# Gated linear attention and a SiLU block: scores computed in halves of a chunk, without the masked block from the ninth chunk on

## The chip, the cores and the metric

The kernel runs on one core of a Trainium2 chip. A core has a matrix engine (PE, whose weight loads are listed as PEld), a vector engine (DVE), an activation engine (ACT), a general engine (POOL) and a queue that issues DMAs (SP). Each takes its own list of instructions in order, and they meet at semaphores. Matmuls read operands from the on-chip memory SBUF and write to the accumulator memory PSUM, which has eight banks of 512 float32 columns on 128 partitions. The metric is device time of one execution in microseconds (us); lower is better.

## The reference

Two stages, all float32. The first is a recurrence for each of 4 x 8 batches and heads over 768 tokens, with head size 48:

```python
for t in range(S):
    state = alpha[:, :, t, :, None] * state + np.einsum('bhd,bhe->bhde', k[:, :, t], v[:, :, t])
    y[:, :, t] = np.einsum('bhd,bhde->bhe', q[:, :, t], state)
```

The second takes `y` as 3072 tokens of 384 features: `h = x @ w_in` (384 x 2048), `g = h * sigmoid(h)`, `g @ w_out` (2048 x 384). The weights arrive as 64-bit floats and are converted on the chip.

## The kernel before

**Chunks.** The tokens are cut into 24 chunks of C = 128 tokens with all 8 heads: 6 positions times 4 batches, position by position. Inside a chunk the recurrence is written as a masked product. With A the running product of alpha, k is multiplied by the decay from its token to the chunk's end (k', tile `kp`), q by the inverse of that (q', tile `qp`), and `scores = k'ᵀ q'` for each head, of which only the part with key token <= query token is wanted. A matmul gives all 128 x 128; DVE multiplies by a mask as it brings the scores from PSUM to SBUF. The state of a batch is decayed by the chunk's whole product and gets `k'ᵀ v` added.

**Layout.** Heads go in four pairs (NP = 4): pair j has head 2j on partitions 0 to 47 and head 2j + 1 on 64 to 111, tokens along the columns. So a score matmul has 48 rows, and the two heads of a pair use the two row halves of PE at once, each with its own PSUM bank (`ps[0]`, `ps[1]`).

**Stages of a chunk** (functions of the chunk's number n):
- `products` (L652): alpha, k, q are brought to this layout, for the first NA = 8 chunks by PE transposes (L669), later by DVE from a tile of 32-token blocks that twelve DMAs fill (`turned`, L650). A DVE scan (L674) runs backward over alpha and gives the decays in tile `u`; L681 multiplies k with it in place, so k' lies in `u`. Column 0 of each pair in `u` is the chunk's whole product (`c["all"]`).
- `quotient` (L688): clamp (`least`, L696), reciprocal (L697), forward scan (L699) into tile `p`, product with q (L704), so q' lies in `p`. In the first eight chunks it is called from `products`.
- `scores` (L706): eight matmuls (L715), two masked copies on DVE (L719), four PE transposes of k' (L723) with one ACT copy (L725), four ACT products that decay the state (L729).
- `values` (L734): transposed outputs by matmuls that use four tiles of 32 output rows at once (L749), 16 with the masked scores and 12 with the state and q'; an ACT copy (L754) puts them into `xt`.
- `states` (L755): 16 small matmuls (L764) and two DVE additions (L770).

`u` and `p` come from pools with two buffers each (`upool`, `ppool`). The five PSUM tiles of a chunk (two for scores, one each for L723, `values`, `states`) rotate over the three banks of `ps_a`.

**The second stage as filler.** The matmuls of the SiLU block are cut into `pieces`: plain products for the first two groups of 512 tokens (L807), a scheme with fewer multiplications and more additions for the others (L830 in, L928 out, with DVE additions at L844, L933 and ACT copies at L836), and one plain output block (L955). `fill(step, slot)` runs pieces until the work done reaches what is due at this point.

**Order.** The loop over `step` writes the stages down in program order: in step n first `scores(n-1)`, then `products(n)`, then `values(n-1)` and `states(n-1)`, then from the ninth chunk on `quotient(n)`, with a `fill` after each of the four slots. Each engine's list is made from this when the program is compiled: what is ready goes first by program order, so independent work can move ahead. A tile of a pool has to wait until the last reader of the buffer's earlier content is done. SP issues loads in such an order too; v is loaded two chunks ahead with one DMA (L479), the blocks of alpha, k, q (L465) one chunk ahead.

**Early buffers.** The pools `raw`, `upp` and `spare` (weights on their way, token tiles of the first eight chunks) are closed by `settle` once the weights are converted; the tiles of the later form (`turn`, the 32-token blocks, ...) take their place. `settle` is tried after slots 1 to 3 of a step from step 7 on.

**Check.** The kernel reads all inputs once more (`audit`, L639) to see whether the quotient form is safe; the result is needed by L1147, late in the program.

Of the kernel before, what the change touches and what calls it, by code (L numbers as in the profile page):

```python
# [8 lines left out]
F32 = mybir.dt.float32  # L9
# [3 lines left out]
AF = mybir.ActivationFunctionType  # L13
ALU = mybir.AluOpType
# [5 lines left out]
def general(  # L20
# [29 lines left out]
    NFT = DF // 128  # L50
    NT = B * NCH
    LEVELS = [1 << i for i in range(7)]
# [255 lines left out]
    for ci in range(NCH):  # L308
        chunks = list(range(ci * B, (ci + 1) * B))
        for pair in (chunks[0:2], chunks[2:4]) if ci == 0 else [[n] for n in chunks]:  # L310
# [10 lines left out]
            for n in pair:  # L321
                if n + NIN < NT:
                    load(n + NIN)
# [32 lines left out]
def quotients(  # L356
# [19 lines left out]
    nc = tc.nc  # L376
    pe, dve, act, gps = nc.tensor, nc.vector, nc.scalar, nc.gpsimd
    B, H, S, D = q.shape
    C = 128
    NCH = S // C  # L380
    NP = H // 2
# [2 lines left out]
    NKT = HD // 128  # L384
    NFT = DF // 128
    NT = B * NCH
    W = C + 1
    GB = 4
    NG = NT // GB
    HF = NFT // 2  # L390
# [4 lines left out]
    def pool(name, bufs=1, space=None):  # L395
        kw = {} if space is None else {"space": space}
        return ctx.enter_context(tc.tile_pool(name=name, bufs=bufs, **kw))

    PS = bass.MemoryType.PSUM
    consts = pool("consts")  # L400
    fix = pool("fix")
# [3 lines left out]
    gpool = pool("gpool", 6)  # L405
    opool = pool("opool", 2)
    rpool = pool("rpool")
    upool = pool("upool", 2)
    ppool = pool("ppool", 2)

    ps_a = pool("ps_a", 3, PS)
    banks = [pool(f"ps_m{i}", 1, PS) for i in range(3)]
# [5 lines left out]
    def ps_attn(n=C):  # L418
        return ps_a.tile([128, 512], F32, name="ps_a").rearrange("p (j c) -> p j c", c=n)
# [5 lines left out]
    ident = consts.tile([128, 128], F32, name="ident")  # L425
# [7 lines left out]
    spare = first.enter_context(tc.tile_pool(name="spare", bufs=1))  # L433
# [4 lines left out]
    NA = 2 * GB  # L438
# [8 lines left out]
    ctxs = {}  # L447
# [26 lines left out]

    def load_v(n):
        c = ctxs.setdefault(n, dict(zip(("ci", "b"), divmod(n, B))))
        rows = slice(c["ci"] * C, c["ci"] * C + C)
        t = c["v"] = vns[n % NV]
        nc.sync.dma_start(t[:, :, 0:D], v[c["b"], :, rows, :].transpose([1, 0, 2]))  # L479

    early = []
    wide = moe_w_in.dtype != F32
# [19 lines left out]

    seg = [(fix if i == 0 else spare).tile([128, NP * W + 1], F32, name=f"al{i}") for i in range(2)]
    inv = fix.tile([128, NP * W + 1], F32, name="inv")
    one = consts.tile([128, NP * W + 1], F32, name="one")
    gps.memset(seg[0], 0.0)
    gps.memset(one, 0.0)
    gps.memset(one[:, 0 : NP * W + 1 : W], 1.0)
    for t in [inv] + seg[1:]:
        gps.memset(t, 0.0)  # L510


    mask = consts.tile([128, C], F32, name="mask")
    gps.memset(mask, 1.0)
    gps.affine_select(mask, mask, pattern=[[1, C]], compare_op=ALU.is_ge, fill=0.0, base=0,
                      channel_multiplier=-1)

    st = [fix.tile([128, NP, 2, D], F32, name=f"st{b}") for b in range(B)]
    for t in st:
        gps.memset(t, 0.0)  # L520
    least = fix.tile([128, NT, NP], F32, name="least")

# [18 lines left out]
    for n in range(NV):  # L541
        load_v(n)
# [99 lines left out]
    xts, xcs, late = {}, {}, {}  # L642

    def tokens(t):

        return t[:, 1 : NP * W + 1].rearrange("p (j c) -> p j c", c=W)[:, :, 0:C]

    def turned(x, to):
        x = x[:, 32:].rearrange("p (g j d) -> p g j d", j=4, d=D)
        dve.transpose(to.rearrange("p g (b j) -> p g j b", j=4), x[:, :, :, 0:32])  # L650

    def products(n):  # L652

        c = ctxs[n]
        sg = seg[0 if late else n % 2]
        ps = {}

        for name in ("a", "k", "q"):
            if n >= NA:
                if name == "a":  # L660
                    turned(c[name], tokens(sg))
                continue
            if n < GB and name != "a":

                ps[name] = out_bank("kq".index(name), 512).rearrange("p (j c) -> p j c", c=C)
            else:
                ps[name] = ps_attn()
            for j in range(NP):
                pe.transpose(ps[name][:, j, :], c[name][:, 2 * j : 2 * j + 2, :], ident)  # L669
            if name == "a":  # L670
                act.copy(tokens(sg), ps[name])  # L671
        end = NP * W
        u = upool.tile([128, end + 1], F32, name="u")
        dve.tensor_tensor_scan(u[:, end - 1 :: -1], sg[:, end:0:-1], one[:, end:0:-1],  # L674
                               0.0, ALU.mult, ALU.add)

        kp = c["kp"] = u[:, 1 : end + 1].rearrange("p (j c) -> p j c", c=W)[:, :, 0:C]
        if n >= NA:
            ps["k"] = late["turn"].tile([128, NP, C], F32, name="turn")
            turned(c["k"], ps["k"])  # L680
        dve.tensor_tensor(kp, ps["k"], kp, ALU.mult)  # L681
        c["all"] = u[:, 0:end:W]
        if n >= NA:
            c["sg"] = sg
        else:
            quotient(n, sg, ps["q"])

    def quotient(n, sg=None, q=None):  # L688

        c = ctxs[n]  # L690
        if sg is None:
            if n < NA:
                return
            sg = c.pop("sg")
        end, iv = NP * W, inv
        dve.tensor_single_scalar(least[:, n, :], c["all"], 2.0**-64, ALU.max)  # L696
        dve.reciprocal(iv[:, 0:end:W], least[:, n, :])  # L697
        p = ppool.tile([128, end + 1], F32, name="p")
        dve.tensor_tensor_scan(p[:, 0:end], sg[:, 0:end], iv[:, 0:end], 0.0, ALU.mult, ALU.add)  # L699
        qp = c["qp"] = tokens(p)  # L700
        if q is None:
            q = late["turn"].tile([128, NP, C], F32, name="turn")
            turned(c["q"], q)
        dve.tensor_tensor(qp, q, qp, ALU.mult)  # L704

    def scores(n):  # L706
        c = ctxs[n]
        ci, b = c["ci"], c["b"]
        ps = [ps_attn() for _ in range(2)]


        for j in range(NP):
            for u in range(2):
                r = slice(64 * u, 64 * u + D)
                pe.matmul(ps[u][:, j, :], lhsT=c["kp"][r, j, :], rhs=c["qp"][r, j, :],  # L715
                          start=True, stop=True)
        g = c["g"] = work.tile([128, 2, NP, C], F32, name="g")
        for u in range(2):
            dve.tensor_tensor(g[:, u], ps[u], mask[:, None, :].to_broadcast([128, NP, C]), ALU.mult)  # L719
        if ci < NCH - 1:  # L720
            ps_k = ps_attn()
            for j in range(NP):
                pe.transpose(ps_k[:, j, :], c["kp"][:, j, :], ident)  # L723
            c["kn"] = work.tile([128, NP, C], F32, name="kn")
            act.copy(c["kn"], ps_k)  # L725
        if ci > 0:
            s = st[b].rearrange("p j u e -> p j (u e)")
            for j in range(NP):
                act.mul(s[:, j], s[:, j], c["all"][:, j : j + 1])  # L729

# [285 lines left out]
    conv_done = [0, 0]  # L1016
# [51 lines left out]
    done, bridged = 0, 0  # L1068
    STEPS = NT + 1
    SLOTS = 4  # L1070
# [31 lines left out]
    for step in range(STEPS):  # L1102
        stages = [[(scores, 1)], [(products, 0)], [(values, 1)], [(states, 1)]]
        if step < GB:

            stages = stages[1::-1] + stages[2:]
        elif step >= NA:
            stages = [[(scores, 1)], [(products, 0)], [(values, 1), (states, 1)], [(quotient, 0)]]
        for slot, group in enumerate(stages):
            for stage, lag in group:  # L1110
                n = step - lag
                if not 0 <= n < NT:
                    continue
                stage(n)
                if stage is values:
                    bridged = n + 1
                if stage is products and n + NIN < NA:
                    load(n + NIN)
                if stage is quotient and n + 1 < NT:
                    load(n + 1)  # L1120
                if stage is states and n + NV < NT:
                    load_v(n + NV)
            fill(step, slot)
            if step >= NA - 1 and slot > 0 and conv_done[1] == NFT and not late:
                settle()
    turns = 0
    while next(audits, 0) is None:
# [10 lines left out]
    for i, (x, op, bound, holds) in enumerate(checks):  # L1138
        e = ends[:, i : i + 1]
        dve.tensor_reduce(e, x, axis=AX, op=op)  # L1140
        dve.tensor_single_scalar(e, e, bound, holds)  # L1141
    good = work.tile([128, 1], F32, name="good")
# [1 line left out]
    go_on()  # L1144
    go_on()
    ps = ps_attn()[0:1, 0, 0:1]
    pe.matmul(ps, lhsT=good, rhs=mask[:, C - 1 : C], start=True, stop=True)  # L1147
    dve.tensor_single_scalar(small, ps, 127.5, ALU.is_ge)
    for _ in range(4):
        go_on()  # L1150
# [60 lines left out]
```

## Time and profile before

| | us |
|---|---|
| median of 5 runs (lowest to highest) | 573.2 (572.31 to 574.53) |
| the profiled execution's own time | 574.4 |
| its span, first to last instruction | 572.7 |
| matmuls L928 (two forms), sum of their busy time | 122.7 + 91.6 |
| matmuls L807, 128 x 256 | 89.8 |
| scores L715, 384 records | 28.6 |
| values L749, 768 + 480 records | 28.8 + 17.0 |
| DVE transposes L650, 48 | 18.1 + 17.9 + 17.7 |

The mean granted clock of PE is 0.991. A float32 matmul appears as two records, a transpose as one. Busy time of a line is the time in which at least one of its instructions ran; the mean of one is longer where several run side by side. A timeline merges neighbours of one line and gives start, length, engine, line, tiles and how many; an entry in brackets is idle time ahead of it and what ended it. In the list of DMA issues, vn takes 3.4 us from issue to landing, the 32-token blocks 2.3 to 2.8.

### The profile page before, as it was taken

To read this page: it belongs to the slowest core of one execution; us is meant where nothing else is said; L and a number is where in the kernel's file an instruction comes from. 1 tells how busy PE (TensorE), PEld (TensorE's weight loads), DVE (VectorE), ACT (ScalarE), POOL (GpSimd) and SP (SyncE) were. 2 spreads that over 40 slices of the span, in tenths; PEclk is the share of its full clock that TensorE was granted. 3 is DMA by queue.
4 is the path that set the end of the run, shared out by engine and by line. 5 is a ranking of instruction groups with operands and counts; after the bars stand their busy time and mean duration, and the time that the engine had idled before them with its cause. 6 is when DMAs were issued, how large, how long until landed. Compare 5 with 4: busy or idle time off the path is not lost. (4 is left out here: it accounts for less than half of the span.)

```text
span 572.7 us, 11703 instructions
## 1 busy us (share of the span) xinstructions
PE 553.2 (97%) x4770; PEld 490.9 (86%) x4770; DVE 449.2 (78%) x807; ACT 187.4 (33%) x367; POOL 7.3 (1%) x25
## 2 busy tenths in 40 slices
PE   5889999999999999999999999999999999999986
PEld 3777887678999999899999999999898999998986
DVE  5879799899798699996997996997962866756751
ACT  2345443233211232442433442423432341423100
POOL 5000000000000000000000000000000000000000
PEclk9799999999999999999999999999999999999998
DMA  9997785336434414443324332324210113333320
GB/s 213 170 289 216 201 215 135 94 97 152 115 91 122 128 46 104 129 112 81 109 56 129 113 106 77 114 50 113 64 39 15 52 52 117 117 96 126 97 76 28
DMA packets 93903, 63.77 MB, mean 111 GB/s; under 512 B 54800, under 2 KB 85520, under 8 KB 93840
## 3 DMA queue, kind: packets, MB, share of 16 engines
q1 hardware_dynamic: 93840, 62.94, 41.8%
q8 instruction: 39, 0.64, 0.5%
q14 instruction: 24, 0.20, 0.1%
HBM read 58.20 MB, written 4.72 MB: 110 GB/s over the span
## 5 line engine op out<-in xcount | busy, mean ns | idle before, releaser
L928 PE MATMUL ps_o<-w_out,g 128*128 128x192 f32 x704 | 122.7, 328 | 1.4 <-DVE o L942 1.3
L928 PEld LDWEIGHTS ps_o<-w_out,g 128*128 128x128 f32 x704 | 115.3, 190 | 4.3 <-DVE o L942 1.7
L928 PE MATMUL ps_o<-wt,g 128*128 128x192 f32 x528 | 91.6, 326 | 0.1
L807 PE MATMUL ps_m<-xt,w_in 128*128 128x256 f32 x384 | 89.8, 384 | 1.7 <-DVE w_in L604 1.0
L928 PEld LDWEIGHTS ps_o<-wt,g 128*128 128x128 f32 x528 | 87.2, 190 | 1.7 <-DVE u L1004 0.4
L807 PEld LDWEIGHTS ps_m<-xt,w_in 128*128 128x128 f32 x384 | 70.7, 190 | 13.1 <-DVE w_in L604 3.4
L830 PE MATMUL ps_m<-xc,w_in 128*128 128x256 f32 x288 | 70.1, 379 | 0.3 <-DVE g L844 0.3
L639 DVE TENSOR_REDUCE seen<-bits 128x1 f32<-128x384 int32 (+2 forms) x65 | 42.4, 689 | 26.6 <-DMA bits<-in_moe_w_out_dram 21.0
L830 PEld LDWEIGHTS ps_m<-xc,w_in 128*128 128x128 f32 x288 | 54.0, 190 | 6.8 <-DVE g L844 0.6
L830 PE MATMUL ps_m<-xc,wx 128*128 128x256 f32 x192 | 50.1, 383 | 0.0
L836 ACT COPY g<-ps_m 128x512 f32<-128x512 f32 x64 | 36.9, 586 | 39.1 <-PE ps_m L830 39.1
L933 DVE TENSOR_TENSOR g<-g 128x512 f32<-128x512 f32 x66 | 44.7, 687 | 4.7 <-PE ps_o L928 4.7
L841 ACT ACTIVATE g<-g 128x1024 f32<-128x1024 f32 x32 | 33.2, 1056 | 43.8 <-DVE g L844 43.8
L729 ACT ACTIVATE st<-st,u 128x96 f32<-128x96 f32 x80 | 25.9, 368 | 54.1 <-DVE u L674 38.9
L844 DVE TENSOR_TENSOR g<-ps_m,g 128x512 f32<-128x512 f32 x56 | 37.6, 682 | 2.9 <-PE ps_m L830 2.7
L830 PEld LDWEIGHTS ps_m<-xc,wx 128*128 128x128 f32 x192 | 35.0, 190 | 4.2 <-issue 0.4
L719 DVE TENSOR_TENSOR g<-ps_a,mask 128x512 f32<-128x512 f32 x48 | 31.2, 685 | 6.2 <-PE ps_a L715 5.9
L674 DVE TENSOR_TENSOR_SCAN u<-al,one 128x516 f32<-128x516 f32 x24 | 29.3, 1222 | 5.4 <-ACT al L671 5.4
L699 DVE TENSOR_TENSOR_SCAN p<-al,inv 128x516 f32<-128x516 f32 x24 | 29.5, 1229 | 4.8 <-PE ps_a L749 4.2
L836 ACT COPY part<-ps_m 128x512 f32<-128x512 f32 x32 | 18.7, 586 | 43.4 <-PE ps_m L830 38.1
L810 ACT ACTIVATE g<-ps_m 128x512 f32<-128x512 f32 x32 | 19.0, 593 | 41.0 <-PE ps_m L807 40.7
L749 PE MATMUL ps_a<-g,vn 128*32 128x128 f32 x768 | 28.8, 282 | 1.9 <-DVE g L719 1.9
(117 smaller groups left out, 630.6 us busy)
## 6 DMA issues: line engine op xcount, KB each, us to landing
bits<-in_moe_w_in_dram SPq DMA_DIRECT2D x24, 512.0 KB, 4.1
bits<-in_moe_w_out_dram SPq DMA_DIRECT2D x32, 384.0 KB, 3.2
at<-in_alpha_dram SPq DMA_DIRECT2D x64, 96.0 KB, 2.3
kt<-in_k_dram SPq DMA_DIRECT2D x64, 96.0 KB, 2.8
qt<-in_q_dram SPq DMA_DIRECT2D x64, 96.0 KB, 2.6
vn<-in_v_dram SPq DMA_DIRECT2D x24, 192.0 KB, 3.4
bits<-in_alpha_dram SPq DMA_DIRECT2D x9, 512.0 KB, 3.6
out_dram<-o SPq DMA_DIRECT2D x48, 96.0 KB, 1.8
```

The lines of the kernel that those rows point to most:

```text
L639: dve.tensor_reduce(seen[kind][which][:, i : i + 1], x, axis=AX, op=op, apply_absolute_value=True))
L674: dve.tensor_tensor_scan(u[:, end - 1 :: -1], sg[:, end:0:-1], one[:, end:0:-1], 0.0, ALU.mult, ALU.add)
L699: dve.tensor_tensor_scan(p[:, 0:end], sg[:, 0:end], iv[:, 0:end], 0.0, ALU.mult, ALU.add)
L719: dve.tensor_tensor(g[:, u], ps[u], mask[:, None, :].to_broadcast([128, NP, C]), ALU.mult)
L749: pe.matmul(py[32 * at : 32 * at + 32, t, :], lhsT=w, rhs=x, start=(i < 4), stop=(i >= len(todo) - 4), skip_group_check=True)
L807: pe.matmul(ps[:, e, :], lhsT=w_in[:, t, (f + e) * 128 : (f + e + 1) * 128], rhs=xt[:, t, :], start=(t == 0), stop=(t == NKT - 1))
L830: pe.matmul(ps[:, e], lhsT=block_w(w)[:, 2 * pair + e], rhs=block_x(grp, x), start=(first and e == 0), stop=(e == 1), skip_group_check=True)
L836: act.copy(to, ps)
L841: act.activation(x, x, AF.Silu)
L844: dve.tensor_tensor(to, a, b, op)
L928: pe.matmul(ps, lhsT=x, rhs=w[:, i], start=(first and i == 0), stop=(i == HF - 1), skip_group_check=True)
L933: dve.tensor_tensor(cells(grp, h, pair, *to), cells(grp, h, pair, *x), cells(grp, h, pair, *y), ALU.subtract)
```

## The change

A score matrix has four blocks of 64 x 64, of which the one with late keys and early queries is masked off whole. The scores are now computed by sixteen matmuls with 64 keys each instead of eight with 128, and from the ninth chunk on those of the late keys stream the 64 late queries alone. For pairs 2 and 3 (four heads) the two halves of the keys change places: k' is written with its halves swapped, v is loaded with its halves swapped, and the mask has a second form. The PSUM cells that no matmul writes are set to zero by ACT beforehand (`blank`), since the masked copy reads them. k' no longer lies in `u` but in a tile of its own, so that the product with the decay is two instructions; k' and q' have two buffers in turn for the first eight chunks and one from then on. The clamp `least` moves to `products`, and the state's decay reads it. `settle` cannot come before the last slot of step 7.

```diff
-    upool = pool("upool", 2)
-    ppool = pool("ppool", 2)
+    upool = pool("upool")
...
-        nc.sync.dma_start(t[:, :, 0:D], v[c["b"], :, rows, :].transpose([1, 0, 2]))
+        nc.sync.dma_start(t[:, 0 : H // 2, 0:D], x[:, 0 : H // 2])
+        for e in range(2):
+            nc.sync.dma_start(t[CH * e : CH * e + CH, H // 2 :, 0:D], x[CH - CH * e : C - CH * e, H // 2 :])
...
+    kps = [(spare if i else fix).tile([128, NP, C], F32, name=f"kp{i}") for i in range(2)]
+    qps = [(spare if i else fix).tile([128, NP * W + 1], F32, name=f"p{i}") for i in range(2)]
+
+    def turns(x, n):
+
+        return x[(n + 1) % 2 if n < NA else 0]
...
-    mask = consts.tile([128, C], F32, name="mask")
+    mask = consts.tile([128, 2, C], F32, name="mask")
     gps.memset(mask, 1.0)
-    gps.affine_select(mask, mask, pattern=[[1, C]], compare_op=ALU.is_ge, fill=0.0, base=0,
-                      channel_multiplier=-1)
+    for odd in range(2):
+        for e in range(2):
+            m = mask[CH * e : CH * e + CH, odd, :]
+            gps.affine_select(m, m, pattern=[[1, C]], compare_op=ALU.is_ge, fill=0.0,
+                              base=-CH * (e ^ odd), channel_multiplier=-1)
...
-        kp = c["kp"] = u[:, 1 : end + 1].rearrange("p (j c) -> p j c", c=W)[:, :, 0:C]
+        dve.tensor_single_scalar(least[:, n, :], u[:, 0:end:W], 2.0**-64, ALU.max)
+        kp = c["kp"] = turns(kps, n)
+        ut = tokens(u)
...
-        dve.tensor_tensor(kp, ps["k"], kp, ALU.mult)
-        c["all"] = u[:, 0:end:W]
+        j = NP // 2
+        dve.tensor_tensor(kp[:, 0:j], ps["k"][:, 0:j], ut[:, 0:j], ALU.mult)
+        k, ut = [x[:, j:].rearrange("p j (e c) -> p j e c", e=2) for x in (ps["k"], ut)]
+        dve.tensor_tensor(kp[:, j:].rearrange("p j (e c) -> p j e c", e=2)[:, :, ::-1], k, ut, ALU.mult)
...
-        dve.tensor_single_scalar(least[:, n, :], c["all"], 2.0**-64, ALU.max)
         dve.reciprocal(iv[:, 0:end:W], least[:, n, :])
-        p = ppool.tile([128, end + 1], F32, name="p")
+        p = turns(qps, n)
...
+    def blank(n):
+
+        if n < NA:
+            return
+        ps = ctxs[n]["blank"] = [ps_attn() for _ in range(2)]
+        for t in ps:
+            act.activation(t.rearrange("p j c -> p (j c)"), ident[:, 0:1].to_broadcast([128, 4 * C]),
+                           AF.Copy, scale=0.0)
...
-        for j in range(NP):
-            for u in range(2):
-                r = slice(64 * u, 64 * u + D)
-                pe.matmul(ps[u][:, j, :], lhsT=c["kp"][r, j, :], rhs=c["qp"][r, j, :],
-                          start=True, stop=True)
+        for j in (0, 2, 1, 3):
+            for e in range(2):
+                for u in range(2):
+                    r = slice(64 * u, 64 * u + D)
+                    at = slice(CH * e, CH * e + CH)
+                    t = slice(CH * (e ^ j // 2) if n >= NA else 0, C)
+                    pe.matmul(ps[u][at, j, t], lhsT=c["kp"][r, j, at], rhs=c["qp"][r, j, t],
+                              start=True, stop=True)
...
-            dve.tensor_tensor(g[:, u], ps[u], mask[:, None, :].to_broadcast([128, NP, C]), ALU.mult)
+            dve.tensor_tensor(g[:, u].rearrange("p (o j) c -> p o j c", o=2),
+                              ps[u].rearrange("p (o j) c -> p o j c", o=2),
+                              mask[:, :, None, :].to_broadcast([128, 2, NP // 2, C]), ALU.mult)
...
-                act.mul(s[:, j], s[:, j], c["all"][:, j : j + 1])
+                act.mul(s[:, j], s[:, j], least[:, n, j : j + 1])
...
-            stages = [[(scores, 1)], [(products, 0)], [(values, 1), (states, 1)], [(quotient, 0)]]
+            stages = [[(scores, 1)], [(products, 0)], [(values, 1), (states, 1)], [(quotient, 0), (blank, 0)]]
...
-            if step >= NA - 1 and slot > 0 and conv_done[1] == NFT and not late:
+            if step * SLOTS + slot >= NA * SLOTS - 1 and conv_done[1] == NFT and not late:
                 settle()
```

CH is 64, half a chunk.

More of the change, by code (lines that the diff above doesn't have):

```diff
@@ L386, in quotients @@
     NT = B * NCH
+    CH = C // 2
     W = C + 1
@@ L476, in load_v @@
         c = ctxs.setdefault(n, dict(zip(("ci", "b"), divmod(n, B))))
-        rows = slice(c["ci"] * C, c["ci"] * C + C)
+        x = v[c["b"], :, c["ci"] * C : c["ci"] * C + C, :].transpose([1, 0, 2])
         t = c["v"] = vns[n % NV]
-        nc.sync.dma_start(t[:, :, 0:D], v[c["b"], :, rows, :].transpose([1, 0, 2]))
+        nc.sync.dma_start(t[:, 0 : H // 2, 0:D], x[:, 0 : H // 2])
+        for e in range(2):
+            nc.sync.dma_start(t[CH * e : CH * e + CH, H // 2 :, 0:D], x[CH - CH * e : C - CH * e, H // 2 :])
     early = []
@@ L708, in scores @@
         ci, b = c["ci"], c["b"]
-        ps = [ps_attn() for _ in range(2)]
-        for j in range(NP):
-            for u in range(2):
-                r = slice(64 * u, 64 * u + D)
-                pe.matmul(ps[u][:, j, :], lhsT=c["kp"][r, j, :], rhs=c["qp"][r, j, :],
-                          start=True, stop=True)
+        ps = c.pop("blank") if n >= NA else [ps_attn() for _ in range(2)]
+        for j in (0, 2, 1, 3):
[6 more added lines that the diff above has]
+                              start=True, stop=True)
         g = c["g"] = work.tile([128, 2, NP, C], F32, name="g")
         for u in range(2):
-            dve.tensor_tensor(g[:, u], ps[u], mask[:, None, :].to_broadcast([128, NP, C]), ALU.mult)
+            dve.tensor_tensor(g[:, u].rearrange("p (o j) c -> p o j c", o=2),
+                              ps[u].rearrange("p (o j) c -> p o j c", o=2),
+                              mask[:, :, None, :].to_broadcast([128, 2, NP // 2, C]), ALU.mult)
         if ci < NCH - 1:
@@ L1146, in quotients @@
     ps = ps_attn()[0:1, 0, 0:1]
-    pe.matmul(ps, lhsT=good, rhs=mask[:, C - 1 : C], start=True, stop=True)
+    pe.matmul(ps, lhsT=good, rhs=mask[:, 0, C - 1 : C], start=True, stop=True)
     dve.tensor_single_scalar(small, ps, 127.5, ALU.is_ge)
```

## The prediction

> **What bounds the kernel now.** I read the page's busy shares first, then the busy time by stretch, then the timeline of one step, then the waits.
>
> Page, part 1 and the head of part 5:
> ```profile
> span 572.7 us, 11703 instructions
> PE 553.2 (97%) x4770; PEld 490.9 (86%) x4770; DVE 449.2 (78%) x807; ACT 187.4 (33%) x367; POOL 7.3 (1%) x25
> ```
> Busy time of each engine in stretches of 40 us (columns PE, PEld, DVE, ACT, POOL, clock, DMA):
> ```profile
> 160.00:200.00 40.00, 40.00 (x390) 36.52 (x389) 31.66 (x60) 9.20 (x20) 0.00 (x0) 1.00 0.45 121
> 200.00:240.00 40.00, 39.28 (x308) 35.46 (x306) 39.65 (x78) 12.95 (x28) 0.00 (x0) 1.00 0.33 92
> 280.00:320.00 40.00, 40.00 (x394) 36.84 (x393) 35.55 (x65) 14.77 (x27) 0.00 (x0) 1.00 0.34 93
> ```
> PE has no idle time in most of the middle, at full clock. So whatever PE time goes away in a late step should leave the total, unless the next engine is late. That engine is DVE: 79 to 89% busy, and 99% from 200 to 240, the one stretch with PE stalls (0.72 us).
>
> Timeline of PE over one step (start, length, line):
> ```profile
> 305.51 1.08 PE L749 MATMUL ps_a<-g,vn 128*32 128x128 f32 x32
> 306.41 0.84 PE L749 MATMUL ps_a<-p,st 128*32 128x128 f32 x24
> 307.07 0.52 PE L764 MATMUL ps_a<-vn,kn 128*32 128x48 f32 x32
> 307.52 1.13 PE L830 MATMUL ps_m<-xc,wx 128*128 128x256 f32 x4
> ...
> 315.50 1.16 PE L715 MATMUL ps_a<-p,u 48*128 48x128 f32 x16
> 316.59 0.66 PE L723 MATMUL ps_a<-ident,u 128*128 128x128 f32 x4
> ```
> A float32 matmul stands as two records. L749 packs four 32-column tiles: 24 records are 6 rounds of four and take 307.07 - 306.41 = 0.66, so 0.110 us per round of 128 columns. The scores (L715) pack two row halves: 16 records are 8 rounds, 0.88 us at that rate, yet the next line starts 1.09 us later. The other 0.21 us lies around the change of tile shape, before and after.
>
> **The change, part by part.**
>
> *Scores on PE.* Eight matmuls with 128 stationary columns become sixteen with 64, so four tiles (two row halves, two column halves) take part. In the first eight chunks each tile still streams 4 x 128 columns in two records each: 8 rounds, nothing gained. From the ninth on, a tile streams 128, 64, 128, 64: in rounds 2 x (1 + 1/2 + 1 + 1/2) = 6, if a tile goes on to its next matmul while its neighbour still streams. Then the stage takes 6 x 0.110 + 0.21 = 0.87 us, 0.22 less, over 16 chunks 3.5 us. If tiles go in step, each round has a long member and nothing is saved. The rows nearest to that question are early ones in which 48-column and 128-column matmuls of the same tile shape overlap:
> ```profile
> 24.66 0.30 PE L749 MATMUL ps_a<-g,vn 128*32 128x128 f32 x3
> 24.70 0.21 PE L764 MATMUL ps_a<-vn,kn 128*32 128x48 f32 x1
> 24.74 0.86 PE L749 MATMUL ps_a<-g,vn 128*32 128x128 f32 x23
> 25.34 0.29 PE L764 MATMUL ps_a<-vn,kn 128*32 128x48 f32 x4
> 25.43 0.27 PE L749 MATMUL ps_a<-g,vn 128*32 128x128 f32 x1
> 25.43 0.21 PE L764 MATMUL ps_a<-vn,kn 128*32 128x48 f32 x1
> ```
> Four short ones start between 25.34 and 25.43 while long ones are still under way and another long one starts after them. A tile that goes at its own pace does this; tiles in step would not. I take 3.5, with 0 as the other end.
>
> A rule speaks against it. The Trainium skill, "TensorE: Matmul & The Clock Gate", Part 3 (row and column tiling), says that matmuls are strictly first-in first-out, in start and in end. By that a tile that is free early waits for the earlier instruction to start: with the written order of heads (0, 2, 1, 3) the last tile ends after 7 rounds, the gain is estimated at 0.11 x 16 = 1.8 us, and the sum below would come to 572.7. The interleaved rows are nearer to the case, so I stay with 6 rounds.
>
> *Blanking.* Two ACT copies of 512 columns into PSUM per late chunk; such copies take 0.58 us (kn, L725), so 1.2 us per step of 21 on an engine that is 33% busy. They use banks whose last reader is ACT itself (kn, then xt), so ACT blocks on nothing new; they are written in front of a slot of filler work, which lasts 8 us on PE (307.52 to 315.50). Cost 0 while that cover stands; without it, up to 1.2 us per step. The wait of the first score for ACT adds at most one sequencer entry: 0.05 x 16 = 0.8; I count 0, the filler ahead covers it.
>
> *k times its decay in two halves (L681).* One 512-element product of 0.69 us becomes two of 256; xc rows of 256 take 0.41 and start 0.34 apart, so the pair holds DVE for about 0.68 where the one held 0.61: 0.07 x 24 = 1.7 us of DVE, beside PE except in the start and in the saturated stretch. The clamp (L696, 0.17) only moves ahead. The mask product has the same element count: 0.
>
> *Buffers.* k' gets a tile of its own, and from the ninth chunk k' and q' have one buffer each instead of two. So the k' product waits for the transposes of the chunk before (L723, at the step's start; it is needed a whole step later: 0), and the quotient scan (L699) waits for the values of the chunk before, no longer of the one before that. Behind L699 on DVE are the q' product (L704) and all later DVE work of the fillers; scores wait for L704. From the end of L749 (307.3) to L715 (315.50) there are 8.2 us; scan and product need 1.23 + 0.69. In the worst step that I found, five microseconds of sums stand ahead:
> ```profile
> 284.35 0.84 PE L749 MATMUL ps_a<-p,st 128*32 128x128 f32 x24
> 290.71 1.23 DVE L699 TENSOR_TENSOR_SCAN p<-al,inv 128x516 f32<-128x516 f32 x1
> 292.17 0.69 DVE L704 TENSOR_TENSOR p<-turn,p 128x512 f32<-128x512 f32 x1
> 293.45 1.16 PE L715 MATMUL ps_a<-p,u 48*128 48x128 f32 x16
> ```
> There the product would end at 292.86, 0.6 us ahead of the scores. So the new wait just fits. I count 0.5 us for the whole run, from 0 to the rival's price.
>
> *v in three DMAs.* SP issues two more per chunk, 0.39 each, with 12 loads of 0.43, stores and reads of the audits in a step of 21 us: hidden, since v is loaded more than a step ahead. At the start four more stand in front of the third chunk's loads: 4 x 0.39 = 1.6 us. Bytes are the same, and the DMA engines are the limit there (busy share 9 tenths or more), so I take half, 0.8; ends 0 and 1.6. The four mask selects and the larger memset on POOL (0.29 each, about 1 us) end long before the first mask product at 14.7: 0.
>
> *Loads of the ninth chunk.* The close of the early buffers moves two slots later, and the region now holds q' of the seventh chunk, read until 107.3. Twelve loads of 0.43 after that are 5.2 us, plus 2.5 to land: about 115. The ninth chunk's q' cannot be written before the eighth's values end (121.9) anyway, and its scores start at 127.4: 0.
>
> Sum on the profiled execution: 574.4 (span 572.7 and 1.7 around it) - 3.5 + 0.8 + 0.5 = 572.2. That execution is 1.2 above the median of the runs, so the median goes from 573.2 to 571.0.
>
> **The rivals.**
>
> *The quotient comes late (slower).* Place: L699 to L704, in each of 16 steps. For it: DVE is 85% busy, and a queue in order puts other late products in front; the measured slack was 0.6 us at the worst step. Against it: 8.2 us of cover in a usual step, with 1.9 needed. It decides once PE waits more than 2.2 / 16 = 0.14 us per step; at 0.35 it costs 5.6 and gives 571.0 - 0.5 + 5.6 = 576.1.
>
> *DVE becomes the bound in its full stretches.* For it: 99% from 200 to 240 and 36.17 of 40 us from 360 to 400. Some 5.5 of 16 steps would then save nothing (1.2 us lost) and the 0.07 per chunk counts there (0.4): 572.6.
>
> *Tiles go in step.* The scores take 8 rounds as before; only the costs stay: 573.2 + 1.3 = 574.5. The rows at 25.34 speak against it, though they show 32-column tiles, not halves of rows and columns at once.
>
> **How the numbers follow.** Forecast as summed 0.52 (its own range 569.4 to 572.0: from all costs at 0 with 0.3 of luck in order, to 0.9 more); late quotient 0.20; DVE bound 0.18; tiles in step 0.10. A measurement of this kernel tells about 0.2%, 1.15 us, so faster means below 572.05 and slower above 574.35. Faster: nearly all of the forecast's 0.52 and a fifth of the DVE case, 0.55. Slower: the late quotient and half of the tiles in step, 0.25. The rest, 0.20. The range from 569.3 to 575.8 leaves out the far part of the late quotient and a little at the lower end.
>
> **What would show it.** Right: score records from the ninth chunk on start the transposes 0.87 us later, not 1.09; PE stays at 40 of 40 us; the scores' idle time names no DVE or ACT; the last scores start about 2 us sooner than 443.0. Wrong: PE idle ahead of the scores put down to L704 or to the blanking; 1.09 us still; a start of the third chunk more than 1.6 us later than 32.3; DVE above 99% in more stretches with PE below 40.

## The result and the profile after

The changed kernel takes 570.95 us (median of 28 runs, 569.73 to 573.56), the kernel before 573.37 (52 runs, 572.12 to 574.99): ratio 0.9963, 95% interval 0.9955 to 0.9971, 2.4 us less. The profiled execution's own time is 573.12 (span 571.4); that of the kernel before was 574.4.

Head of the page of the changed kernel:
```profile
span 571.4 us, 12612 instructions
PE 552.8 (97%) x5154; PEld 488.8 (86%) x5154; DVE 448.9 (79%) x831; ACT 201.9 (35%) x399; POOL 8.4 (1%) x28
```
PE is busy 0.4 us less than before and ACT 14.5 us more (for the most part the blanking copies). The stretches shown before, now (columns PE, PEld, DVE, ACT, POOL, clock, DMA):
```profile
160.00:200.00 40.00, 40.00 (x425) 36.57 (x425) 34.42 (x66) 11.24 (x25) 0.00 (x0) 1.00 0.44 118
200.00:240.00 40.00, 38.35 (x334) 34.37 (x332) 39.62 (x80) 14.08 (x29) 0.00 (x0) 0.98 0.39 109
280.00:320.00 40.00, 40.00 (x429) 36.89 (x428) 35.78 (x68) 18.01 (x35) 0.00 (x0) 1.00 0.36 94
```
PE is still full in the first and last, at full clock. In the middle one it has lost 0.93 us more than before, and the clock is no longer 1.00. The lines have moved: scores L715 to L745, transposes of k' L723 to L755, values L749 to L781, states L764 to L796, sums of the expert products L844 to L876.

The timeline of PE over the same late step:
```profile
306.52 0.84 PE L781 MATMUL ps_a<-p,st 128*32 128x128 f32 x24
307.18 0.52 PE L796 MATMUL ps_a<-vn,kn 128*32 128x48 f32 x32
...
315.61 0.90 PE L745 MATMUL ps_a<-p,kp 48*64 48x128 f32 x32
316.44 0.66 PE L755 MATMUL ps_a<-ident,kp 128*128 128x128 f32 x4
```
The scores' stage, from their first record to the next line, takes 316.44 - 315.61 = 0.83 us; before it took 1.09. All chunks from the tenth on show 0.83 (the ninth 0.95, with a wait of 0.20 ahead of it). In the fifth to eighth chunk, where nothing is left out, it takes 1.04:
```profile
97.28 1.10 PE L745 MATMUL ps_a<-p,kp 48*64 48x128 f32 x32
98.32 0.66 PE L755 MATMUL ps_a<-ident,kp 128*128 128x128 f32 x4
```

So the saving is there and no wait took its place at the scores. Where did it go? Compare the starts of the scores, changed minus before. At the fifth chunk (66 us) it is -0.22; at the ninth -0.20; from the tenth on each step adds -0.26, down to -1.39 at 226.37 (before 227.76). The fifteenth chunk's scores start at 251.10, 0.89 **later** than before; then -0.26 per step again down to -1.46 at the last (441.58 against 443.04). Between two steps 2.54 us were lost. The timeline of PE there:
```profile
236.90 1.13 PE L862 MATMUL ps_m<-xc,w_in 128*128 128x256 f32 x4 [1.24 <-DVE g L876]
238.43 1.97 PE L862 MATMUL ps_m<-xt,w_in 128*128 128x256 f32 x4 [0.40 <-DVE g L876]
```
The same two waits in the kernel before:
```profile
237.62 1.13 PE L830 MATMUL ps_m<-xc,w_in 128*128 128x256 f32 x4 [0.32 <-DVE g L844]
239.15 1.13 PE L830 MATMUL ps_m<-xt,w_in 128*128 128x256 f32 x4 [0.40 <-DVE g L844]
```
So PE stalls (stands idle) 0.92 us more. And the second row lasts 1.97 instead of 1.13 us: the granted clock is 0.5 for 3.41 us from 238.6, which costs 1.7. Stalls and clock together are about the 2.5 us. A second profile of the changed kernel, taken beside the later experiments, has the same two stalls and keeps its full clock there:
```profile
238.40 1.13 PE L862 MATMUL ps_m<-xc,w_in 128*128 128x256 f32 x4 [1.24 <-DVE g L876]
239.93 1.13 PE L862 MATMUL ps_m<-xt,w_in 128*128 128x256 f32 x4 [0.40 <-DVE g L876]
```
In it this step takes 23.11 us (scores to scores) where the first profile has 24.73, so the half clock cost 1.6. It also hides the saving in PE's busy time: of the 4.2 us that the scores save, the half clock takes back 1.7, and in the first 40 us PE is busy 2.0 us more than before (32.14 instead of 30.12).

Of the 32 executions of the changed kernel whose mean granted clock is on record beside this result, the 17 with 0.997 or more have a median of 570.6 us, the 15 with less 572.55. Where the clock was low in them is known only for the profiled one.

The step that the prediction called the worst, now (timeline of all engines):
```profile
286.44 1.23 DVE L716 TENSOR_TENSOR_SCAN p<-al,inv 128x516 f32<-128x516 f32 x1
...
291.20 0.68 DVE L721 TENSOR_TENSOR p<-turn,p 128x512 f32<-128x512 f32 x1
...
293.83 0.44 PE L745 MATMUL ps_a<-p,kp 48*64 48x128 f32 x8
```
The product with q ends at 291.88, 1.95 us ahead of the scores, where it was 0.6 before: the scan now stands earlier in DVE's list.

### The profile page after: what moved, and what is told of

Same layout as the page of the kernel before. It is cut to its first block, busy times and chain, and to the rows that moved or that the text cites. A ratio compares the mean times of both kernels' runs of the same rounds, so it can differ in the third digit from the quotient of the medians.

```text
span 571.4 us, 12612 instructions
## 1 busy us (share of the span) xinstructions
PE 552.8 (97%) x5154; PEld 488.8 (86%) x5154; DVE 448.9 (79%) x831; ACT 201.9 (35%) x399; POOL 8.4 (1%) x28
## 5 line engine op out<-in xcount | busy, mean ns | idle before, releaser
L653 DVE TENSOR_REDUCE seen<-bits 128x1 f32<-128x384 int32 (+2 forms) x65 | 42.4, 687 | 27.0 <-DMA bits<-in_moe_w_out_dram 21.2
L761 ACT ACTIVATE st<-st,least 128x96 f32<-128x96 f32 x80 | 24.1, 365 | 44.5 <-DVE least L691 44.5
L876 DVE TENSOR_TENSOR g<-ps_m,g 128x512 f32<-128x512 f32 x56 | 37.9, 685 | 2.4 <-PE ps_m L862 2.2
L749 DVE TENSOR_TENSOR g<-ps_a,mask 128x512 f32<-128x512 f32 x48 | 31.2, 685 | 9.4 <-PE ps_a L745 9.0
L781 PE MATMUL ps_a<-g,vn 128*32 128x128 f32 x768 | 29.3, 284 | 0.0
L781 PEld LDWEIGHTS ps_a<-g,vn 128*32 128x32 f32 x768 | 20.9, 113 | 8.9 <-issue 6.7
```

Source lines behind the costliest of these rows:

```text
L653: dve.tensor_reduce(seen[kind][which][:, i : i + 1], x, axis=AX, op=op, apply_absolute_value=True))
L749: dve.tensor_tensor(g[:, u].rearrange("p (o j) c -> p o j c", o=2), ps[u].rearrange("p (o j) c -> p o j c", o=2), mask[:, :, None, :].to_b ...
L781: pe.matmul(py[32 * at : 32 * at + 32, t, :], lhsT=w, rhs=x, start=(i < 4), stop=(i >= len(todo) - 4), skip_group_check=True)
L876: dve.tensor_tensor(to, a, b, op)
```

## The experiments

Each ratio is to runs of the kernel before on the same chip; its medians there are 574.12 in the first four, 576.03 in the next four, 575.63 in the three after them, 576.22 in the last. Nearly every edit also makes the compiler write the engines' lists in a somewhat different order, and this turned out to matter as much as the edits did.

### The order of the pairs

```diff
-        for j in (0, 2, 1, 3):
+        for j in range(NP):
```


> The changed kernel with the four pairs in the order 0, 1, 2, 3 instead of 0, 2, 1, 3, so that a tile gets 128, 128, 64, 64 columns and its neighbour 64, 64, 128, 128. Theory (each tile goes at its own pace): still 6 rounds, stage 0.83 us, time as the changed kernel, 571.0. Rival (matmuls start in program order, a free tile waits): 8 rounds, stage 1.04 us, time 574.4. A queue of limited depth would lie between, 0.9 to 1.0 us.

Measured: 571.44, ratio 0.9953 (0.9939 to 0.9967). Timeline of PE:
```profile
291.63 0.94 PE L745 MATMUL ps_a<-p,kp 48*64 48x128 f32 x32
292.50 0.66 PE L755 MATMUL ps_a<-ident,kp 128*128 128x128 f32 x4
```
The stage takes 0.87 us, 0.04 more per step than in the other order; six rounds either way, where eight take 1.04 in the early chunks. By the rule of the Trainium skill ("TensorE: Matmul & The Clock Gate", Part 3), that matmuls start and end strictly in order, the changed kernel's order would take an estimated 7 rounds and this one 8. The rule does not hold here: tiles of 48 x 64 go on at their own pace. The single records of the changed kernel's stage at 315.61 say it too, read by their column counts: pair 2's late keys (128 columns) start at 315.79, ahead of its early keys (64 columns, 315.88), which come first in the program.

### All 128 queries for the late keys

This kernel does the masked block's work again in every chunk; the rest is as changed.
```diff
-                    t = slice(CH * (e ^ j // 2) if n >= NA else 0, C)
+                    t = slice(0, C)
```


> The changed kernel, but the score matmuls of the late keys stream all 128 queries in every chunk (the masked block is computed again; the sixteen half-width matmuls, the swap, the blanking and the single buffers stay). All theories agree that the score stage of a late chunk then takes 8 rounds: 1.04 us from its first record to the first transpose, as the changed kernel's early chunks show, where the changed kernel has 0.83. If the gain is PE time of that block, the time rises by 16 x 0.21 = 3.4 us over the changed kernel, to about 574.4, a little above the kernel before. If the gain came from elsewhere (the start, the order of work), it stays near 571.

Measured: 574.44, ratio 1.000 (0.999 to 1.001); stage 1.04 in every chunk. Against 0.9963, the left-out block is worth 2.1 us in all, though 16 x 0.21 = 3.4 leave PE. On this chip the run above, which leaves the block out too, is 3.0 us faster (571.44). The stalls near 237, timeline of PE:
```profile
237.33 1.13 PE L862 MATMUL ps_m<-xc,w_in 128*128 128x256 f32 x4 [0.76 <-DVE g L876]
238.86 1.13 PE L862 MATMUL ps_m<-xt,w_in 128*128 128x256 f32 x4 [0.41 <-DVE g L876]
```
The first is 0.76 here and 1.24 with the block left out: 0.48 more, about two steps' saving (2 x 0.21). Counted from the fifth chunk's scores, leaving the block out brings PE there 1.28 us earlier, but DVE's sum only 0.80. This execution's clock stays at full speed there.

### The masked block left out, but no swap

v comes in one DMA, k' (still in two products) and the mask are in plain order; the late keys' matmuls stream 64 queries in all four pairs.
```diff
-        nc.sync.dma_start(t[:, 0 : H // 2, 0:D], x[:, 0 : H // 2])
-        for e in range(2):
-            nc.sync.dma_start(t[CH * e : CH * e + CH, H // 2 :, 0:D], x[CH - CH * e : C - CH * e, H // 2 :])
+        nc.sync.dma_start(t[:, :, 0:D], x)
...
-                              base=-CH * (e ^ odd), channel_multiplier=-1)
+                              base=-CH * e, channel_multiplier=-1)
...
-        dve.tensor_tensor(kp[:, j:].rearrange("p j (e c) -> p j e c", e=2)[:, :, ::-1], k, ut, ALU.mult)
+        dve.tensor_tensor(kp[:, j:].rearrange("p j (e c) -> p j e c", e=2), k, ut, ALU.mult)
...
-                    t = slice(CH * (e ^ j // 2) if n >= NA else 0, C)
+                    t = slice(CH * e if n >= NA else 0, C)
```


> The changed kernel without the swap of halves: k', v and the mask as in the kernel before (one DMA for v, one mask form in both places), the masked block still left out in the late chunks. Every early-key tile then streams 128 columns four times, every late-key tile 64. Theory (own pace, the fullest tile ends last): 8 rounds, stage 1.04 us, time 574 or a little less since v is one DMA. Rival (the stage goes by all columns streamed): 0.83 us and 571 or less.

Measured: 576.32, ratio 1.0034 (1.0019 to 1.0050). The stage takes 1.02 us: the tiles of the early keys still stream 4 x 128 queries, and they set the end. So without the swap there is next to nothing to gain (1.04 where all is streamed). That it is slower than before has another cause, on ACT and then PE at the ninth chunk:
```profile
136.00 0.37 ACT L759 ACTIVATE st<-st,least 128x96 f32<-128x96 f32 x1 [3.33 <-DVE least L689]
136.28 0.58 ACT L840 ACTIVATE g<-ps_m 128x512 f32<-128x512 f32 x1
```
```profile
136.91 1.35 PE L837 MATMUL ps_m<-xt,w_in 128*128 128x256 f32 x5 [1.50 <-ACT g L840]
```
In this build ACT's list has a decay of the state (it waits for `least` from DVE) ahead of an expert's activation; PE's next product waits for that activation. In the changed kernel the third such activation stands before the decay (134.01 against 137.70) and PE does not wait. The rest is 0.6 us in the start (the fifth chunk's scores at 66.80, before 66.19) and 3.41 us of half clock at 530, behind a stall of 1.88.

### Two buffers for q'

```diff
-    qps = [(spare if i else fix).tile([128, NP * W + 1], F32, name=f"p{i}") for i in range(2)]
+    qps = [fix.tile([128, NP * W + 1], F32, name=f"p{i}") for i in range(2)]
...
-        return x[(n + 1) % 2 if n < NA else 0]
+        return x[(n + 1) % 2 if n < NA or x is qps else 0]
```


> The changed kernel with two buffers for q' in all chunks, so that the quotient scan waits only for the values of the chunk before the last. Theory (the lost lead of the quotient makes DVE late where it is full): PE's idle time around 237 us falls from 1.24 + 0.40 towards the 0.32 + 0.40 of the kernel before, the granted clock stays up behind it, and the median falls by 0.5 to 1.5 us, to 569.5 to 570.5. Rival (DVE is simply full there, whatever the buffers): idle time and median as in the changed kernel, 571.0 within 0.4.

Measured: 574.18, ratio 0.9989 (0.9973 to 1.0005), and not the improvement expected. The eleven executions lie in two groups, three at 570.8 to 571.6 and eight at 573.5 to 574.8; the first three have a mean granted clock of 0.997 to 1.000, the eight 0.988 to 0.997. The profiled one is of the first. In it PE waits 0.92 us at 134.51 for ACT, as in the run above, and the stall behind the sums (L876) has moved to 226.38 and grown to 1.84. The wait of 0.20 at the ninth chunk is gone. So giving the buffer back does not take the stall away; as DVE's list is another one here too, this run alone does not say what made it grow.

### One buffer for q' in the kernel before

```diff
-    ppool = pool("ppool", 2)
+    ppool = pool("ppool", 1)
```


> The kernel before with one change alone: q' gets one buffer in all chunks in place of two. It asks what the lost buffer costs by itself. Theory (the single buffer is nearly free, the 0.5 us of the prediction): 0 to 0.5 us above the kernel before, ratio 1.000 to 1.001, and PE's idle time ahead of the scores (L715) put down to the q' product stays under 0.1 us per step. Rival one (late quotient): 0.14 us or more per step, 2.2 us or more in all, ratio 1.004 or more. Rival two (the buffer's loss is what made the stall near 237 us grow): the stall of the expert's matmuls there goes from 0.32 to about 1.2 us, 0.9 us more, and by 1.7 more where the granted clock is then halved for 3.4 us; ratio about 1.002 to 1.003.

Measured: 578.06, ratio 1.0039 (1.0024 to 1.0055). PE never waits for the q' product at the scores, so the late quotient is not it, though the size of the ratio was its forecast. Timeline of PE:
```profile
100.67 0.66 PE L669 MATMUL ps_a<-ident,an 128*128 128x128 f32 x4 [0.99 <-DVE g L719]
...
238.88 1.13 PE L830 MATMUL ps_m<-xc,w_in 128*128 128x256 f32 x4 [0.46 <-DVE g L844]
```
0.99 us are lost in an early chunk, where the mask product stands behind weight conversions in DVE's list; the changed kernel has two buffers there and no such wait. From the ninth chunk on this build loses 0.4 us, all between 228 and 251 us. The first stall there is 0.46, not 1.2: the second rival falls as well. About 1 us of the 2.25 is left; the stalls after 480 us add up to 4.4 us here and to 2.9 in the profile of the kernel before, which is of another chip.

### No blanking

The form with all 128 queries again, where no cell is left unwritten, so that the blanking can go.
```diff
-        ps = c.pop("blank") if n >= NA else [ps_attn() for _ in range(2)]
+        ps = [ps_attn() for _ in range(2)]
```


> The changed kernel in the form in which the late matmuls of the second key half stream all 128 queries again, now also without the blanking copies on ACT (every cell is written, so none is needed). Beside the form with blanking (574.44 us) it gives the price of the blanking. Theory (hidden): the same time within 0.6 us; ACT's busy time falls by 16 x 2 x 0.58 = 18.6 us, stage of the scores 1.04 us. Rival (the blanking delays ACT's other copies and so PE and DVE): 1 us or more below 574.44, with the stall near 237 us smaller than 0.76.

Measured: ratio 0.9994 (0.9984 to 1.0005) beside 1.000 (0.999 to 1.001) with blanking. ACT is busy 185.0 instead of 202.6 us, and the stalls near 237 are 0.75 and 0.40 (0.76 and 0.41 with it). Within the intervals the blanking is hidden.

### v in three DMAs, in the kernel before

```diff
-        nc.sync.dma_start(t[:, :, 0:D], v[c["b"], :, rows, :].transpose([1, 0, 2]))
+        x = v[c["b"], :, rows, :].transpose([1, 0, 2])
+        nc.sync.dma_start(t[:, 0 : H // 2, 0:D], x[:, 0 : H // 2])
+        for e in range(2):
+            nc.sync.dma_start(t[(C // 2) * e : (C // 2) * (e + 1), H // 2 :, 0:D], x[(C // 2) * e : (C // 2) * (e + 1), H // 2 :])
```


> The kernel before with one change alone: v comes in three DMAs per chunk (four heads whole, then the two row halves of the other four), without the swap. It asks for the price of the two more DMAs, above all in the start. Theory of the prediction: the third and fourth chunk's loads are issued up to 1.6 us later, the scores that started at 66.19 us start 0.8 us later, ratio about 1.001 to 1.002. Rival (the start is not set by the order of SP's issues): these scores start within 0.3 us of 66.19 or earlier, ratio 0.999 to 1.000.

Measured: 580.37, ratio 1.0080 (1.0055 to 1.0104), worse than either forecast. The scores of the fifth chunk start at 68.68, 2.49 later. Before that, between 34 and 37 us, PE and DVE:
```profile
34.34 0.66 PE L726 MATMUL ps_a<-ident,u 128*128 128x128 f32 x4
36.89 0.38 PE L752 MATMUL ps_a<-g,vn 128*32 128x128 f32 x2 [1.90 <-issue]
```
```profile
36.11 0.68 DVE L722 TENSOR_TENSOR g<-ps_a,mask 128x512 f32<-128x512 f32 x1
```
PE waits 1.90 us. The profile names no releaser, but the mask product whose result this matmul reads ends at 36.79; two weight conversions, a product with k and a clamp stood ahead of it in DVE's list. Then the clock is 0.5 for 3.41 us from 37.0. Later, at 139, PE waits 1.66 us for ACT, as in the run without the swap, and at 534 2.23 us for DVE, with a half clock behind it. None of these waits is put down to a DMA. The changed kernel issues the same DMAs and its fifth chunk starts 0.22 us earlier than before. The part alone has no price that could be added to others; the list that it led to has one.

### Less for DVE to do where it is full

From the ninth chunk on the kernel reads part of its inputs once more per step and reduces it on DVE (the audit, 1.21 us at this stage, L653). Two of them move from the full stretch to the end.
```diff
-        if late and at % 4 == 0:
+        if late and at % 4 == 0 and step not in (13, 14):
```


> The changed kernel with the audits of the input (one reduction of 1.21 us on DVE per step) left out in the thirteenth and fourteenth step and made later, so that DVE has 2.4 us less to do between 205 and 251 us; nothing is left undone. Theory (DVE is full there, so that its queue is late for the expert's products, and the stall there brings the half clock): the stalls of 1.24 and 0.40 us near 237 fall to 0.4 or less together, no half clock near 239, scores of the fifteenth chunk start 1.2 us or more earlier than 251.1, median 569.3 to 570.0, ratio about 0.993. Rival (the stall is a matter of the order in which DVE's list was written, not of its load): the stall stays or turns up in a neighbouring step, median 570.6 to 571.5.

Measured: 571.14, ratio 0.9918 (0.9904 to 0.9933), so 2.6 us better than the change alone (0.9963, on other chips). Both stalls near 237 are gone, no half clock follows, and the fifteenth chunk's scores start at 247.49 instead of 251.10; at the last scores the lead over the kernel before is 5.08 us. Part of it is lost again at the end, where two more audits wait (timeline of PE, rows with idle time):
```profile
516.66 1.13 PE L862 MATMUL ps_m<-xt,wx 128*128 128x256 f32 x4 [0.93 <-DVE g L876]
524.62 3.25 PE L960 MATMUL ps_o<-w_out,g 128*128 128x192 f32 x16 [1.63 <-DVE o L974]
546.18 2.87 PE L960 MATMUL ps_o<-w_out,g 128*128 128x192 f32 x16 [2.06 <-DVE o L974]
```
From 440 us on one audit follows the other every 4.2 us or so, since there is one buffer for their data, and DVE stands still for each DMA (27.0 us in all in the changed kernel); the products of the output wait behind them.

### The same edit in the kernel before

The condition on the audits as above, in the kernel before.

> The kernel before with the audits left out in the thirteenth and fourteenth step and made later, nothing else. It asks whether the full stretch of DVE cost the kernel before as much as the changed one. Theory (DVE's load there eats what PE saves): the kernel before gains only its two stalls of 0.32 and 0.40 us and loses about as much in the tail, ratio 0.999 to 1.002, where the changed kernel gained some 2.6 us by the same edit. Rival (the edit is good by itself and has nothing to do with the change): the same 2 to 3 us, ratio 0.995 to 0.997.

Measured: 575.19, ratio 0.9996 (0.9984 to 1.0008). Its two stalls vanish too (its scores start 1.26 us earlier from there on), and the tail takes it back. The changed kernel gained 2.6 us by the same edit: the full stretch had cost it far more.

### The audits spread, and the changed kernel beside it

```diff
-        if late and at % 4 == 0:
+        if late and (at % 4 == 0 and step not in (13, 14) or at % 4 == 2 and step >= 20):
```


> The changed kernel with the audits left out in the thirteenth and fourteenth step, as in the run before it, and with a second audit per step in the last five steps, so that the list of audits ends three audits earlier than in the changed kernel and not two later. Nothing is left undone. Theory (late audits hold up the end: from 440 us on each takes about 4.2 us, the wait for its DMA included, and PE's stalls in the tail are stalls behind them): the gain near 237 us stays, PE's stalls after 480 us fall from the 5.5 us of the run before to 2.5 or less, and the time is 2 to 4 us below the changed kernel on the same chip, 0.5 to 2.5 us below the run before. Rival (DVE has no room in the last steps either, or the tail is set by PE's own work): a stall of 0.5 us or more turns up between 380 and 460 us and the time is not below that of the run before.

> The changed kernel itself once more, beside the others on one chip, so that they can be compared with it: ratio to the kernel before 0.995 to 0.997.

Measured: 567.38, ratio 0.9859 (0.9845 to 0.9873). The changed kernel itself: 573.87, 0.9970 (0.9953 to 0.9988), so the spread audits are worth 6.5 us by the medians. Part of this is the clock: all four executions with spread audits have a mean granted clock of 0.999 or more, nine of the twelve of the changed kernel less than 0.997; the other three have a median of 572.6, which leaves 5.2 us. Window from 200 to 240 and the stalls of PE in the tail:
```profile
200.00:240.00 40.00, 39.93 (x425) 36.36 (x424) 38.71 (x79) 15.95 (x32) 0.00 (x0) 1.00 0.34 90
```
```profile
485.83 2.87 PE L960 MATMUL ps_o<-w_out,g 128*128 128x192 f32 x16 [0.43 <-DVE o L974]
521.75 3.25 PE L960 MATMUL ps_o<-w_out,g 128*128 128x192 f32 x16 [0.19 <-DVE o L974]
533.63 0.19 PE L1179 MATMUL ps_a<-mask,good 128*1 128x1 f32 x2 [1.48 <-DVE good L1175]
```
Counting stalls of 0.15 us or more, there are 2.1 us after 480 instead of 5.5 in the run with two late audits. No stall turns up between 380 and 460, though DVE is at 37.91 of 40 us from 360 to 400. The changed kernel's second profile shows the stalls of 1.24 and 0.40 near 237 again, to the hundredth, but full clock after them; its half clock lies in the start (10.2 us from 16.8), and its fifth chunk's scores start 1.29 us later than in the kernel before.

### The same placing in the kernel before

> The kernel before with the audits placed as in the best version (none in the thirteenth and fourteenth step, two per step in the last five), nothing else. Beside the best version (ratio 0.9859) it shows what the change is worth where neither the full stretch of DVE nor the audits at the end take anything back. Theory (all of PE's saving then leaves the total): 16 x 0.26 + 4 x 0.06 - 0.2 at the ninth chunk = 4.2 us, so ratio 0.993 here, no PE stall between 200 and 480 us. Rival (the change is worth its 1.7 to 2.4 us everywhere, and the placing of the audits adds its own gain): ratio 0.989 to 0.990.

Measured: 572.95, ratio 0.9936 (0.9923 to 0.9949), no PE stall between 61 and 480 us. The best version lies 0.0077 below, 4.4 us (give or take 1.1 by the two intervals): where no stall stands in the middle the change is worth 4.4, not 2.4. That is close to what the scores' stage saves (16 x 0.26 = 4.2, and 0.2 in the early chunks), but not all of it comes from there. Between the two profiles, which are of two chips and 6.0 us apart, 3.7 us are gained from the fifth chunk's scores to the end of the last chunk's; 0.6 lie in the start, 0.6 in the stalls of the tail and 1.1 behind PE's last matmul.

## Why the prediction was right, and where it was not

The median came out at 570.95 for a forecast of 571.0, but three terms of the sum were off and cancelled, so that it was met so closely is luck in part. On the profiled execution the sum gave 572.2, and it took 573.12.

- **Scores, -3.5.** The mechanism was right: six rounds, each tile at its own pace, and the skill's rule with seven rounds (572.7) was rightly not taken. The size was too small: the stage is 0.83, not 0.87, so 16 x 0.26 = 4.2. The term mis-sized is the 0.21 us around the change of tile shape; with 48 x 64 tiles eight rounds take 1.04, which leaves 0.16. For the same reason "the first eight chunks: nothing gained" was 0.05 per chunk too low.
- **v in three DMAs, +0.8.** Wrong: a later issue was taken for a later landing. The third chunk's loads begin to be issued 2.1 us later (12.75 instead of 10.66), but the last of them lands at 20.09 instead of 19.90. v of the fourth chunk is issued 1.5 us later (28.80 instead of 27.34) and has landed 0.5 later; no wait for it appears, and the fifth chunk's scores start 0.22 earlier. The start moves with the order of DVE's list and with the clock: 64.6 to 68.7 us for the fifth chunk over all builds, 65.97 and 67.48 for the same build.
- **Single buffers, +0.5.** The place was wrong. The scores never wait for q' except 0.20 at the ninth chunk, where the scan waits 1.44 us for the values of the chunk before, and the worst step has more slack than before. What the change cost was in the full stretch of DVE: 0.92 us more stall, and in one of two profiles a half clock for 1.7.
- **DVE bound, as a rival (572.6).** Its place was right for one stretch of two: 200 to 240 swallows the saving of two steps (0.48), 360 to 400 swallows none at 36.4 of 40. It overlooked that the stall could grow beyond the swallowed saving. Of the growth of 0.92, 0.48 is the scores' saving, about 0.1 the saving of the shape by itself, and 0.14 what one buffer for q' added in the kernel before; some 0.2 was not traced. What the swap brought is not in it (0.77 without, 0.76 with).
- **Blanking, mask, clamp, loads of the ninth chunk at 0.** Blanking was tested and is free. The memsets behind the later q' region wait 100.2 us on POOL; only the DMA queue waits for one of them, 0.4 us. The ninth chunk's loads have landed at 117.2 where about 115 was said. For none of these does PE stand idle.
- **Late quotient (576.1), tiles in step (574.5).** Both refuted, by the stall lists and by 0.83.
- **What would show it.** Stage, idle time of the scores and PE outside the full stretch came as said; "PE stays at 40 of 40" did not hold from 200 to 240; the last scores came 1.46 us sooner where 2 were said, because the fifteenth chunk lost 2.5.

The sum that the runs support: -4.2 scores, -0.2 early chunks, -0.2 start, +0.2 ninth chunk, +0.9 stall near 237, and +1.7 in executions with the half clock there: -3.5 or -1.8. The median's -2.4 lies between. The profiled executions' own times differ by -1.3, which is 0.5 short of the second: 0.3 us are more stall in the tail, the rest is not located.

## What to carry to other kernels

A saving on the full engine leaves the total only where the next engine has room at that very place: look for the one stretch in which it has none, and move optional work (here a 1.2 us reduction per step) out of it; that gave 5 to 6.5 us where the change itself gave 2.4. Test a part by the stage that it changes and by the stall list, not by the total alone: a build in which one line differs can have other lists on all engines, and those moved the total by 2 to 4 us here. Work that is spread "one per step" should be spread by the room there is, and not be left to pile up at the end.

## What was not expected of the hardware

The granted clock falls to 0.5 for 3.41 us, behind short stalls: after 1.24 + 0.40 us of idle time within 2.8 us in one execution, after 1.88, 1.90, 2.13 and 2.23 in others, and not after 1.84 or 2.06, nor after the same 1.24 + 0.40 in another execution. The page "TensorE: Matmul & The Clock Gate" of the Trainium skill (Part 1) has a free-running window of about 3.4 us. The traces agree: in each profile the changes of the clock lie a whole number of 3.413 us apart. Counted in these windows, much of what looks like chance is the place of the stall. The 2.06 us and the second 1.24 + 0.40 are split over two windows, while 1.88, 1.90, 2.13, 2.11 of the 2.23 and the first 1.24 + 0.40 lie in one. It does not settle all: up to 1.84 us in one window passed without a half clock, and the first 1.24 + 0.40 is less than that. The page's table lets an idle window pass before the clock falls; here 1.9 to 2.1 us of one were enough. So a stall of about 2 us can cost 1.7 more, by where it happens to fall.

Four tiles of 48 x 64 that stream 128 and 64 columns in turn finish in the time of the mean: 32 records in 0.83 us, beside 1.04 when all stream 128.
